# At most three loads under way on the sync queue of a one-core attention and mixing kernel

## The chip, the cores and the metric

The kernel runs on one core of a Trainium2 chip. The core has five engines that run side by side: TensorE (PE; its weight loads are listed as PEld), VectorE (DVE), ScalarE (ACT), GpSimd (POOL) and SyncE (SP). SP computes nothing; it issues transfers between the chip's memory (DRAM) and the core's own memory (SBUF). Sixteen DMA engines carry the transfers of all queues. The metric is the time of one execution in microseconds (us). Three runs before the change gave 200.77, 201.28 and 204.06 us; the median is 201.28 us.

## What is computed

There are two parts, the second fed by the first. The first is a recurrence over 768 steps for 4 batches of 8 heads with 40 channels each:

```python
for t in range(S):
    y[:, :, t] = einsum('bhd,bhde->bhe', r_t, state)
    Sa = einsum('bhde,bhe->bhd', state, a_t)
    state = state * w_t - einsum('bhd,bhe->bhde', Sa, b_t) + einsum('bhd,bhe->bhde', v_t, k_t)
```

Its output, seen as x of shape 4 x 768 x 320, goes through a mixing stage:

```python
theta = x @ w_theta
y = w_tok_r @ (x * cos(theta)) + w_tok_i @ (x * sin(theta))   # over the 768 tokens
u = x + y
out = u + maximum(u @ w_ch, 0)
```

The inputs r, k, v, w, a, b are six arrays of 4 x 8 x 768 x 40 numbers of 32 bits. They are the bulk of what is loaded.

## The kernel before, in words

**Tiles.** The 768 steps of a batch are cut into six chunks of 128 steps, so there are 24 chunks in all, each holding all eight heads. Within a chunk the recurrence is turned into matrix products; between chunks a small state is handed on. A batch's mixing stage follows when its six chunks are done, and is interleaved with the recurrence of the next batch. The products over the tokens (line 880, `chunk` in `mix_row`) are the largest group of matmuls.

**Loads.** The functions `load` and `loads` (lines 289 and 461) bring the inputs in. A chunk of one array is 160 KB. It is fetched either alone (line 464), as rows of 40 numbers, that is 160 bytes, or in pairs of chunks (line 480), as runs of 8 x 40 numbers, that is 1,280 bytes, of 320 KB. The first six chunks (`TURNED`) take k, b and a in pairs, the first eight (`RUNS`) take v in pairs, and r always comes in pairs; the rest comes in single chunks. The landing tiles are few: four for w, six for a, four for k and b together, six for v, two pairs for r. A load into a tile waits until the old contents have been read.

**Who reads the loads.** ACT takes the logarithm of w (`lw`, line 508). POOL casts k, b, a, v and r to 16 bits (line 498; the first of them on ACT, line 497), into `z`, `o`, `r` or `v`, or multiplies k, b and a by the decays (line 492, `kb` and `ah`). From there TensorE transposes them (lines 418 and 423).

**Order.** All work is recorded as operations (`plan.add`) and then issued in one long hand-kept list, `ORDER` (line 22). The list fixes the order on each engine. `HOMES` names the banks of the matmuls' memory, `PICK` the operations that take their second choice of engine, and `WARM` places small filler matmuls (line 982). The loop at line 988 goes through the list, runs each operation's function, which issues its instructions, and calls `plan.thin` (line 1000), which drops waits that another wait already covers. Each engine works through its own instructions in order and waits on semaphores for those of others.

**Queues.** SP issues 132 transfers in the list's order: 119 loads and 13 stores of the output (lines 911 and 917). Each of SP's transfers reports its landing on one of eight semaphores ("lanes"), in turn; a transfer waits until the one before it on its lane, eight transfers earlier, has landed. That is the only bound on the transfers under way that the program itself sets. POOL issues 16 loads of its own for the weights of the mixing stage (lines 926 and 934).

Of the kernel before, what the change touches and what calls it, by code (L numbers as in the profile page):

```python
# [16 lines left out]

BANKS = 8
RUNS = 8
TURNED = 6  # L20
LATE = 8
ORDER = [
# [224 lines left out]
def kernel(  # L247
# [41 lines left out]
    def load(i):  # L289
# [3 lines left out]
        def src(ap):  # L293
            return ap[bi, :, ci * C:(ci + 1) * C, :].rearrange("h t d -> t h d")
        if i < TURNED:
            return ([("raw_w", s), raw_w[s], src(w)],)
# [3 lines left out]
                [("raw_a", i % NA), raw_a[i % NA], src(a)]) + (  # L300
                () if i < RUNS else ([("raw_v", i % 6), raw_v[i % 6], src(v)],))

# [109 lines left out]
    def pair(t, g):  # L412
        return t[:, 2 * g:2 * g + 2, :].rearrange("p a b -> p (a b)")
# [14 lines left out]
    def turned(kind, kinde, i, blocks, skeys, dst, dkeys, at="tile", eng="ACT", part=64):  # L428
        p = ("ps", kind, i)
        n = len(blocks)  # L430
        whole = n <= 8
        add("PE", kind, i, lambda: turn(ps(p).bitcast(BF16), blocks), reads=skeys, writes=[p],
            at=at, new=(p, 2), alts=(("PE", lambda: turn_whole(ps(p).bitcast(BF16), blocks)),)
            if whole else (), **quad_cost(4 * n))

        def places(width, source):
            a = part * width // 64
            if len(plan.home[p]) == 2:
                return (dst_of(width).rearrange("p n (a w) -> p a n w", a=2),
                        source[:, :, 0:width * n].rearrange(  # L440
                            "p a (n w) -> p a n w", w=width)[:, :, :, 0:a])
            return (dst_of(width).rearrange("p n (a w) -> p (n a) w", a=2),
                    source[:, 0:2 * width * n].rearrange(
                        "p (n w) -> p n w", w=width)[:, :, 0:a])

        def dst_of(width):
            return dst.bitcast(FP32) if width == 32 else dst

        def words():
            to, source = places(32, ps(p))  # L450
            nc.scalar.copy(out=to, in_=source)  # L451

        def halves():
            to, source = places(64, ps(p).bitcast(BF16))
            nc.vector.tensor_copy(out=to, in_=source)
        alts = [("ACT", words), ("DVE", halves)]
        if eng == "DVE":
            alts.reverse()
        add(alts[0][0], kinde, i, alts[0][1], n * 2 * part, [p], dkeys, at=at, alts=(alts[1],))

    def loads(i):
# [7 lines left out]
        sets = [(r, raw_r[i // 2 % 2], "r")]  # L469
        if i < RUNS:  # L470
            sets.append((v, raw_o[i // 2 % 3], "o"))
        if i < TURNED:
            s = i % 4
# [16 lines left out]
    def product(kind, i, dst, in0, in1, reads, writes, fast):  # L490
        dve = ("DVE", lambda: nc.vector.tensor_tensor(out=dst, in0=in0, in1=in1, op=ALU.mult))
        pool = ("POOL", lambda: nc.gpsimd.tensor_tensor(out=dst, in0=in0, in1=in1, op=ALU.mult))  # L492
        one, two = (dve, pool) if fast else (pool, dve)
        add(one[0], kind, i, one[1], 0, reads, writes, alts=(two,))

    def cast(kind, i, dst, src, reads, writes, fast):
        act = ("ACT", lambda: nc.scalar.copy(out=dst, in_=src))
        pool = ("POOL", lambda: nc.gpsimd.tensor_copy(out=dst, in_=src))
        one, two = (act, pool) if fast else (pool, act)
        add(one[0], kind, i, one[1], 0, reads, writes, alts=(two,))  # L500

    def prep(i):
# [43 lines left out]
        fast = i < 2  # L546
        if i >= TURNED:
            product("kb", i, kb[:, :, :, 0:D], raw_kb[s4],
# [3 lines left out]
                    [("raw_a", i % NA), kwe], [("ah", i % 3)], fast)  # L552
        if i >= RUNS:
            cast("v", i, vb[:, :, 0:D], raw_v[i % 6],
# [3 lines left out]
        parts = [("f" + nm, st) for nm in "kba"]  # L558
        if i < TURNED:
            if i % 2 == 0:  # L560
# [5 lines left out]
        skeys, dkeys = [("kb", i % NKB), ("ah", i % 3)], list(parts)  # L566
        if i >= RUNS:
            blocks += [pair(vb, g) for g in range(G)]
            skeys.append(("v", i % NRV))
            dkeys.append(("vT", st))  # L570
        if i >= TURNED:
            turned("tt", "et", i, blocks, skeys, feat[:, 0:len(blocks)], dkeys)
        if i < RUNS and i % 2 == 0:
            turn_runs("o", i, o_t[i // 2 % 2], raw_o[i // 2 % 3],
# [57 lines left out]
    def turn_runs(nm, i, t, raw, dsts):  # L632
        s = i // 2 % 2
        cast(nm, i, t[:, :, :, 0:D], raw.rearrange("p c (q d) -> p q c d", q=8),
             [run_key(nm, i, 0), run_key(nm, i, 1)], [(nm, s)], i == 0)
        pr = ("ps", "t" + nm, i)
        blocks = [t[:, q].rearrange("p c d -> p (c d)") for q in range(8)]
        add("PE", "t" + nm, i, lambda: turn(ps(pr).bitcast(BF16), blocks),
            reads=[(nm, s)], writes=[pr], new=(pr, 2), **quad_cost(32))
        for x, (dst, dkey) in enumerate(dsts):  # L640
            add("ACT", "e" + nm, i + x, lambda x=x, dst=dst: nc.scalar.copy(  # L641
                out=dst.rearrange("p g (t q) -> p g t q", q=8),
                in_=ps(pr).bitcast(BF16)[:, x, 0:512].rearrange(
                    "p (q t g) -> p g t q", q=8, g=G)),
                592, [pr], [dkey])
# [328 lines left out]
    def fill(count, bank):  # L974
        f = Op()
        f.eng, f.idx, f.new = "PE", f"fill_{len(plan.known)}", None
        f.pre, f.reads, f.writes = [], (), (("ps", "fill", len(plan.known)),)
        plan.home[f.writes[0]] = (bank,)
        made = []
        nc.push_inst_callback(made.append)  # L980
        for _ in range(count):
            nc.tensor.matmul(ps(f.writes[0])[:, 0:128], lhsT=busy, rhs=busy, start=True,
                             stop=True, skip_group_check=True)
        nc.pop_inst_callback()
        plan.thin(tc, f, made)

    table = "lnexp"
    for o in plan.order():
        if o.idx in WARM:
            fill(*WARM[o.idx])  # L990
        if o.table is not None and o.table != table:
            table = o.table
            if table == "lnexp":
                nc.scalar.preload_act_table_set(LN_EXP)
        made = []
        nc.push_inst_callback(made.append)
        if o.fn is not None:
            o.fn()
        nc.pop_inst_callback()
        plan.thin(tc, o, made)  # L1000


# [28 lines left out]
```

## Time and profile before

| | |
|---|---|
| median of three runs | 201.28 us |
| profiled execution | 201.0 us |
| its span, first to last instruction | 199.3 us |
| mean granted TensorE clock | 0.987 |
| moved by DMA | 30.90 MB |
| loads of SP, 160 KB each (single chunks) | 94, of 4.4 to 4.8 us from issue to landing (medians) |
| loads of SP, 320 KB each (pairs of chunks) | 25, of 3.6 to 5.4 us (medians) |

All rows of the profile come from one execution of 201.0 us. The span is shorter by 1.7 us, because starting and ending the program lies outside it. In the lists, L464 is line 464 of the kernel; `out<-in` names the tile written and the tile read; "DMA" as the one waited for means that a transfer had not landed. In the list of waits the three numbers are the total in us, how often, and the longest. The timeline of SP gives for each transfer the time of its issue and how long the issue took; the transfer itself goes on after that. "To landing" is the time from the start of the issue to the last semaphore update. The chain of waits is followed back from the last instruction; it tells which work, end to end, set the length of the span.

### The profile page before, as it was taken

The numbers are of one execution on the slowest core, as the hardware profiler recorded it, in microseconds if no ns is written. First come the engines' busy times: TensorE is split into PE (matmuls) and PEld (weight loads), VectorE is DVE, ScalarE is ACT, GpSimd is POOL, SyncE is SP. The second block draws the span as 40 slices with busy tenths as digits, with TensorE's granted clock in tenths as the row PEclk, the third lists the DMA queues.
The fourth block names the chain that finished last, engine by engine and source line by source line (L and its number), as shares of the span: only waits on it lengthen the run. The fifth ranks groups of instructions, "written<-read, shape, count | busy, mean of one in ns | idle before, by whom it ended". The sixth has DMA issues, their size and how long they took to land.

```text
span 199.3 us, 9590 instructions
## 1 busy us (share of the span) xinstructions
PE 184.5 (93%) x4275; PEld 146.2 (73%) x4275; DVE 160.7 (81%) x265; ACT 160.7 (81%) x293; POOL 144.7 (73%) x171
## 2 busy tenths in 40 slices
PE   7879999895998898999989999999999999999992
PEld 7667787684786777777876877876877877887761
DVE  7599999994899999997988968899996647774252
ACT  3499998994999999887979898799799889894011
POOL 5347472986399999889979997764989898579100
PEclk9999999997899999999999999999999999999998
DMA  5998977999987989879988989989848301002122
GB/s 148 290 327 172 285 152 156 142 185 182 189 143 148 196 149 152 154 160 198 176 183 181 212 169 201 196 153 226 200 101 208 57 28 44 3 3 69 66 92 105
DMA packets 110312, 30.90 MB, mean 155 GB/s; under 512 B 98624, under 2 KB 110272, under 8 KB 110272
## 3 DMA queue, kind: packets, MB, share of 16 engines
q1 hardware_dynamic: 107840, 27.53, 64.7%
q0 software_dynamic: 2432, 2.77, 8.4%
q8 instruction: 33, 0.54, 1.1%
q14 instruction: 7, 0.06, 0.1%
HBM read 29.13 MB, written 3.93 MB: 166 GB/s over the span
## 4 chain that ended last, share of the span: by engine, by line
PE 70%; ACT 10%; DVE 9%; DMA 4%; issue 3%; POOL 1%; SPq 1%; POOLq 0%
PE ps L880 21%; PE ps L418 11%; PE ps L667 10%; PE ps L803 9%; PE ps L826 4%; PE ps L423 3%; DMA raw_v<-in_v_dram 2%; DVE lam L675 2%; PE ps L723 2%; DVE phi L675 2%; PE ps L744 2%; DMA raw_kb<-in_k_dram 2%; PE ps L711 2%; PE ps L706 2%; PE ps L517 2%
## 5 line engine op out<-in xcount | busy, mean ns | idle before, releaser
L880 PE MATMUL ps<-z,wtok 128*128 128x320 bf16 x288 | 48.6, 299 | 0.0
L675 DVE TENSOR_TENSOR lam<-ps,mask_p 128x1024 bf16<-128x1024 f32 x31 | 37.7, 1220 | 5.9 <-PE ps L667 5.6
L492 POOL TENSOR_TENSOR z<-cs,xp 128x640 bf16<-128x640 f32 x22 | 30.5, 1402 | 7.5 <-ACT cs L858 7.5
L880 PEld LDWEIGHTS <-wtok 128*128 128x128 bf16 x288 | 24.2, 97 | 8.7
L492 POOL TENSOR_TENSOR kb<-raw_kb,ex 128x640 bf16<-128x640 f32 x18 | 25.7, 1432 | 1.3 <-PE ps L826 0.5
L675 DVE TENSOR_TENSOR phi<-ps,mask_n 128x1024 bf16<-128x1024 f32 x19 | 23.0, 1219 | 3.2 <-PE ps L667 3.2
L675 DVE TENSOR_TENSOR psi<-ps,mask_p 128x1024 bf16<-128x1024 f32 x17 | 20.7, 1217 | 2.6 <-PE ps L667 2.6
L667 PEld LDWEIGHTS <-feat 64*128 64x128 bf16 x576 | 18.0, 95 | 6.1 <-issue 3.0
L677 ACT ACTIVATE lam<-ps 128x1024 bf16<-128x1024 f32 x17 | 17.4, 1026 | 3.6 <-PE ps L667 3.6
L679 POOL TENSOR_SCALAR_AFFINE_SELECT lam<-lam 128x1024 bf16<-128x1024 bf16 x17 | 18.6, 1095 | 0.8 <-ACT lam L677 0.7
L667 PE MATMUL ps<-feat 64*128 64x128 bf16 x384 | 17.8, 219 | 1.2 <-ACT feat L451 0.5
L826 PE MATMUL ps<-kb,lam 128*128 128x40 bf16 x384 | 15.9, 180 | 0.6 <-issue 0.5
L492 POOL TENSOR_TENSOR ah<-raw_a,ex 128x320 bf16<-128x320 f32 x18 | 14.6, 809 | 2.3 <-ACT ex L539 1.5
L826 PEld LDWEIGHTS <-lam 128*128 128x128 bf16 x384 | 13.9, 96 | 1.2 <-issue 0.6
L641 ACT COPY rT<-ps 128x512 bf16<-128x512 bf16 x24 | 13.9, 595 | 0.7 <-PE ps L418 0.7
L890 DVE TENSOR_TENSOR up<-ps,xp 128x640 bf16<-128x640 f32 x11 | 9.0, 822 | 5.3 <-PE ps L880 5.2
L451 ACT COPY feat<-ps 128x1024 f32<-128x1024 f32 (+1 forms) x13 | 12.9, 1002 | 0.5 <-PE ps L418 0.3
L451 ACT COPY uT<-ps 128x384 f32<-128x384 f32 (+1 forms) x9 | 4.0, 447 | 11.3 <-PE ps L423 7.7
L508 ACT ACTIVATE lw<-raw_w 128x320 bf16<-128x320 f32 x24 | 11.4, 479 | 1.8 <-DMA raw_w<-in_w_dram 1.8
L914 DVE SCALAR_TENSOR_TENSOR oo<-ps,up 128x640 f32<-128x640 f32 x11 | 9.0, 822 | 4.5 <-PE ps L803 4.5
L667 PE MATMUL ps<-rT,nuT 64*128 64x128 bf16 x192 | 9.7, 219 | 2.8 <-issue 2.4
L820 PE MATMUL ps<-gd,rT 128*128 128x80 bf16 x80 | 12.3, 197 | 0.0
(156 smaller groups left out, 542.9 us busy)
## 6 DMA issues: line engine op xcount, KB each, us to landing
raw_w<-in_w_dram SPq DMA_DIRECT2D x24, 160.0 KB, 4.6
raw_r<-in_r_dram SPq DMA_DIRECT2D x12, 320.0 KB, 5.0
out_dram<-oo SPq DMA_DIRECT2D x11, 320.0 KB, 3.2
raw_a<-in_a_dram SPq DMA_DIRECT2D x18, 160.0 KB, 4.8
raw_kb<-in_b_dram SPq DMA_DIRECT2D x18, 160.0 KB, 4.6
raw_kb<-in_k_dram SPq DMA_DIRECT2D x18, 160.0 KB, 4.7
raw_v<-in_v_dram SPq DMA_DIRECT2D x16, 160.0 KB, 4.4
raw_v<-in_v_dram SPq DMA_DIRECT2D x4, 320.0 KB, 5.2
```

Of the source, the lines that this page charges most:

```text
L418: nc.tensor.transpose(out=dst[:, c, n * 64:n * 64 + 64], in_=block[rows(c)], identity=ident[rows(c), rows(c)])
L451: nc.scalar.copy(out=to, in_=source)
L492: pool = ("POOL", lambda: nc.gpsimd.tensor_tensor(out=dst, in0=in0, in1=in1, op=ALU.mult))
L641: add("ACT", "e" + nm, i + x, lambda x=x, dst=dst: nc.scalar.copy(out=dst.rearrange("p g (t q) -> p g t q", q=8), in_=ps(pr).bitcast(BF16) ...
L667: nc.tensor.matmul(t[:, q, g, :], lhsT=lhs[rows(q), g, :], rhs=rhs[rows(q), g, :], start=True, stop=True)
L675: add("DVE", kindm, i, lambda: nc.vector.tensor_tensor(out=flat, in0=whole(), in1=mask.to_broadcast([128, 2 * G, 128]), op=ALU.mult), 1217 ...
L677: 1217, [p], dkeys, alts=(("ACT", lambda: nc.scalar.mul(out=flat, in_=whole(), mul=sign)),))
L679: add(None, "sel", i, None, 0, dkeys, dkeys, alts=(("POOL", lambda: nc.gpsimd.affine_select(out=flat, in_=flat, pattern=[[0, 2 * G], [1, 1 ...
L803: nc.tensor.matmul(out, lhsT=lhs[:, 3 * c + kt, :], rhs=wt[:, kt, :], start=kt == 0, stop=kt == 2)
L820: nc.tensor.matmul(t[:, g * 80:g * 80 + 80], lhsT=rT[:, g, :], rhs=gd[:, 2 * g:2 * g + 2, :], start=True, stop=False, skip_group_check=True)
L826: nc.tensor.matmul(t[:, h * D:h * D + D], lhsT=lam[:, n, p, g, :], rhs=kb[:, n, h, 0:D], start=first and n == 0, stop=n == 1, skip_group_c ...
L880: nc.tensor.matmul(to, lhsT=wtok[t % NCH][:, c, s, :], rhs=z[:, c, s], start=s == 0 and c == 0, stop=s == NT - 1 and c == 1)
```

## The change

Every load on SP, from the fourth on, gets one more dependency: on the landing of the third load ahead of it in the same queue. The list of loads is kept in `flight`. Stores on SP and the loads that POOL issues are neither counted nor held. The order of the operations, their banks and their engines stay the same.

```diff
+INFLIGHT = 3
...
+    flight = []
     for o in plan.order():
...
         if o.fn is not None:
             o.fn()
         nc.pop_inst_callback()
         plan.thin(tc, o, made)
+        if o.eng == "SP" and o.kind[0] == "l":
+            if len(flight) >= INFLIGHT:
+                tc.add_manual_dep(made[0], flight[-INFLIGHT].name, mybir.DependencyInfo(
+                    mybir.DependencyClass.Sync, mybir.DependencyReason.DATA),
+                    reason="loads in flight")
+            flight.append(made[0])
```

In the built program the lists of instructions of PE, DVE, ACT and POOL are the same as before, waits included. On SP the order is the same too. Each load waits for the lane of the third load ahead of it, and the old wait on its own lane is gone where the new one covers it, as it nearly always does. The stores lose their lane waits as well, with four exceptions near the end.

## The prediction

> **What bounds the kernel now.** I read the page first, then the chain of waits, then the list of who waited for whom, cut at 36 us, and last the issues of the sync queue (SP) one by one, because the change touches only them.
>
> ```profile
> span 199.3 us, 9590 instructions
> PE 184.5 (93%) x4275; PEld 146.2 (73%) x4275; DVE 160.7 (81%) x265; ACT 160.7 (81%) x293; POOL 144.7 (73%) x171
> q1 hardware_dynamic: 107840, 27.53, 64.7%
> PE 70%; ACT 10%; DVE 9%; DMA 4%; issue 3%; POOL 1%; SPq 1%; POOLq 0%
> ```
>
> PE carries 70% of the chain and DMA 4%, about 8 us. But q1, the queue that SP fills, uses 64.7% of the time of 16 DMA engines over the span, and the loads end well before the kernel does. So where they run, the DMA engines are nearly full. The table by stretch (length, busy time of the five engines, granted clock, DMA share, GB/s) says where:
>
> ```profile
> 8.00:24.00 16.00, 14.05 (x336) 11.16 (x335) 15.02 (x20) 15.85 (x32) 8.14 (x11) 1.00 1.02 270
> 80.00:148.00 68.00, 67.25 (x1560) 51.78 (x1552) 60.14 (x83) 58.72 (x103) 57.85 (x64) 1.00 0.94 183
> 165.00:199.00 34.00, 30.45 (x466) 22.91 (x466) 18.46 (x25) 16.90 (x32) 15.83 (x15) 0.98 0.15 50
> ```
>
> DMA share is 1.02 at the start and 0.94 in the middle, while PE is busy 67.25 of 68.00 us there. In the last 34 us hardly a load is left (0.15), so the change can't act there. Who waits for loads, up to 36 us and then after it:
>
> ```profile
> POOL o L498 <- DMA raw_v<-in_v_dram: 6.3, 2, 5.2
> POOL z L498 <- DMA raw_kb<-in_k_dram: 3.7, 2, 1.9
> POOL z L498 <- DMA raw_kb<-in_b_dram: 3.2, 2, 3.0
> POOL z L498 <- DMA raw_a<-in_a_dram: 2.5, 2, 1.7
> ACT z L497 <- DMA raw_kb<-in_b_dram: 2.2, 1, 2.2
> ```
>
> ```profile
> POOL r L498 <- DMA raw_r<-in_r_dram: 1.1, 1, 1.1
> POOL kb L492 <- DMA raw_kb<-in_b_dram: 0.4, 1, 0.4
> POOL v L498 <- DMA raw_v<-in_v_dram: 0.3, 1, 0.3
> ```
>
> Up to 36 us these five sum to 17.9 us; from there to 160 us all DMA waits sum to 1.8 us. Loads therefore set the pace at the start, and arrive just early enough later.
>
> **The change, part by part.** It adds no instruction of work and moves none: each load's own issue waits until the third load ahead of it has landed. Stores are not counted and get no such wait. Behind a waiting load stand all later loads and stores, since SP issues in order; every consumer on ACT and POOL waits for them. The old waits on a reused completion lane, eight transfers back, fall away, and they cost nothing, being long over.
>
> How many loads are under way now follows from these rows of SP's timeline (start, duration of the issue) and of the list of issues in windows holding one load each (last number: us from issue to landing):
>
> ```profile
> 0.80 0.72 SPq L480 DMA_DIRECT2D raw_kb<-in_b_dram  x1
> 1.58 0.61 SPq L480 DMA_DIRECT2D raw_kb<-in_k_dram  x1
> 2.24 0.60 SPq L464 DMA_DIRECT2D raw_w<-in_w_dram  x1
> 2.88 0.60 SPq L480 DMA_DIRECT2D raw_a<-in_a_dram  x1
> ...
> 18.81 0.61 SPq L480 DMA_DIRECT2D raw_a<-in_a_dram  x1
> ```
>
> ```profile
> raw_kb<-in_b_dram SPq DMA_DIRECT2D x1, 320.0 KB, 3.5
> raw_kb<-in_k_dram SPq DMA_DIRECT2D x1, 320.0 KB, 3.7
> raw_a<-in_a_dram SPq DMA_DIRECT2D x1, 320.0 KB, 4.8
> raw_w<-in_w_dram SPq DMA_DIRECT2D x1, 160.0 KB, 4.5
> ```
>
> ```profile
> raw_a<-in_a_dram SPq DMA_DIRECT2D x1, 320.0 KB, 4.6
> ```
>
> Call the loads 0, 1, 2, ... The first lands at 0.80 + 3.5 = 4.3, the next at 5.3, load 2 at 6.7, and load 3, issued at 2.88, at 7.7. With the change load 3 is issued at 4.3, 1.4 us later. Whether it also lands later depends on how long a load takes when little is ahead of it. Two rows, from windows with one transfer each, bound that: a 160 KB load issued near 25 us, after SP had waited for a buffer, and a store near 163 us that had the DMA engines to itself:
>
> ```profile
> raw_w<-in_w_dram SPq DMA_DIRECT2D x1, 160.0 KB, 2.6
> ```
>
> ```profile
> out_dram<-oo SPq DMA_DIRECT2D x1, 320.0 KB, 2.3
> ```
>
> So of the 4.5 to 5 us that a load now takes, about 2 are time in the queue, and that part can be given up for nothing. Three under way at C us each land one every C/3.
>
> *First stretch, to 24 us.* From load 3 (7.7) to load 19 (18.81 + 4.6 = 23.4) there are 16 loads in 15.7 us: 0.98 each, 2.94 per three. With C = 2.6 the wait is hidden (0.87 each). With C = 3.5, load 0's own time and its size, each takes 1.17 and load 19 lands 3.0 later. These loads are mostly of 320 KB; between 2.6 and 3.5 I take the middle, 3.05: 1.02 each, +0.6 at load 19. To this I add 0.2, because a semaphore is complete only when the slowest of 16 engines is, and the quicker ones then run dry sooner. Not all reaches the chain: in 8:24 ACT is busy 15.85 of 16.00 us, and it covers part of the delay as long as the chain runs through it. Taken: **+0.5**; ends 0 and +2.5.
>
> *The raw_v load at 28.80.* It stands in the chain by itself:
>
> ```profile
> 28.39 0.37 SPq L464
> ...
> 28.80 4.90 DMA raw_v<-in_v_dram
> ...
> 33.76 1.39 POOL o L498 x2
> ```
>
> ```profile
> 25.40 0.74 SPq L480 DMA_DIRECT2D raw_r<-in_r_dram  x1
> ...
> 28.80 1.86 SPq L480 DMA_DIRECT2D raw_v<-in_v_dram  x1
> ```
>
> ```profile
> raw_r<-in_r_dram SPq DMA_DIRECT2D x1, 320.0 KB, 5.4
> ```
>
> The third load ahead of it is raw_r, landing at 25.40 + 5.4 = 30.8. Now the issue runs from 28.80 to 30.66, for 1.86 us where a free one after a wait takes 0.37: the hardware itself holds SP until the queue has room. With the change it runs from 30.8 to 31.2, so it ends 0.5 later, not 2. If raw_r lands later too, up to 1 more. POOL has nothing else to do (it waited 5.2), so all of it goes to the chain: **+0.8**, ends 0 and +1.6.
>
> *From 36 us on.* Long issues show that the hardware does already most of what the change asks for:
>
> ```profile
> 52.67 0.58 SPq L464 DMA_DIRECT2D raw_w<-in_w_dram  x1
> 53.29 3.00 SPq L464 DMA_DIRECT2D raw_v<-in_v_dram  x1
> 56.38 0.66 SPq L464 DMA_DIRECT2D raw_kb<-in_k_dram  x1
> ```
>
> The issue at 53.29 hung for 3.00 us. What the loads need here, from the queue's row for 100:148:
>
> ```profile
> q1 hardware_dynamic: 39903, 8.85, 91.2%
> ```
>
> 8.85 MB are as much as 54 transfers of 160 KB in 48 us: one every 0.89 us, three every 2.67. A load with little ahead takes 2.6, plus 0.05 for SP to wake (my estimate, from raw_v: it landed at 28.80 + 4.90 = 33.70, and POOL began at 33.76): 2.65. That is as tight as it can be without loss. About every second load would be issued later than now by up to 0.7, and three consumers had no slack at all, as the waits of 1.1, 0.4 and 0.3 show. Taken: **+1.0** for those and for the slip behind them; ends 0 and +6 (second rival).
>
> The profiled execution took 201.0 us, 1.7 around its span; the median of the three runs is 201.28, so the sum holds for both. 201.0 + 0.5 + 0.8 + 1.0 = **203.3 us**.
>
> A rule speaks against these additions. The Trainium skill ("DMA: Bandwidth & Descriptors", section "Anatomy of one DMA — SWDGE (gpsimd) path") gives a transfer a fixed part of about 2.0 us plus bytes at 436 GB/s; that is given for another kind of queue, and an estimate from it is 2.4 us for 160 KB and 2.8 for 320 KB. The trace's 2.6 and 2.3 lie near it. By it three loads land every 2.4 to 2.8 us, less than 2.94 at the start, and the sum would be about +0.5, the first rival below.
>
> **The rivals.** *It costs nothing.* For it: the long issues (1.86, 3.00), which mean that a fourth load is only half in the queue anyway, and C = 2.6. Against it: the first rows, in which load 3's issue at 2.88 isn't held at all, and raw_v's 0.5. Time: 201.0 + 0.5 = 201.5. That the wait isn't there at all would give the same time; but in the built program each load from the fourth on names the lane of the third ahead of it, and the lists of the other engines are as before.
>
> *The queue runs dry.* Place: 80 to 148 us, DMA share 0.94, so 4 us in 68 are free to make up for gaps. It decides from C over 2.67: at 3.05, my value for the start, three loads take 0.38 longer, and the 54 transfers of 100:148 slip by 18 x 0.38 = 6.8 us. With a little from 80:100 and from the start, and about 2 us of slack ahead of most consumers taken off, +7: 208. For it: no spare share, PE in a fixed order, and 16 DMA engines that don't finish together. Against it: a wait that replaces a hung issue (3.00) adds only the difference.
>
> *Faster.* Instruction loads and POOL's weight loads share the DMA engines, and a shorter SP queue could let them by. A wait of PE, and q8, the queue of the instruction loads, over the span and then in 165:199:
>
> ```profile
> PE ps L667 <- issue: 2.4, 1, 2.4
> ```
>
> ```profile
> q8 instruction: 33, 0.54, 1.1%
> ```
>
> ```profile
> q8 instruction: 4, 0.07, 0.9%
> ```
>
> PE once sat 2.4 us with nothing to wait for but its own issue; the chain has 3% of "issue", 6 us. Halved, that gives 198. Against it: an instruction packet takes 0.011 x 16 x 199.3 / 33 = 1.06 us over the span and 0.009 x 16 x 34 / 4 = 1.2 in 165:199, where SP's queue is nearly empty, so the queue doesn't slow the packet itself. The Trainium skill ("DMA: Bandwidth & Descriptors", section "Queues, rings and completion order") says that a DMA engine takes turns between queues packet by packet, so a deep SP queue would hold another queue up by one packet only; by this rule nothing is gained.
>
> **How the numbers follow.** The forecast, +1 to +6 around 203.3, gets 0.45; 2% of the median is 4.0 us, about what a measurement of this kernel can tell from no change, so some 0.13 of it lies over 205.3. No cost: 0.18. The queue runs dry, 204.5 to 213: 0.30, all but a sliver slower. Faster: 0.07, of which 0.05 is under 197.3. That gives slower 0.43, same 0.52, faster 0.05. The range leaves out the faster case and the top third of the dry queue: 200.0 to 209.0.
>
> **What would show it.** Right: median time to landing of the 160 KB loads falls to 3 to 3.5; hung issues vanish and SP's own waits name raw loads; POOL's waits for loads up to 36 us grow from 15.7 by 1 to 2; raw_v lands near 34.5; DMA share in 80:148 stays over 0.9. Wrong: if DMA share there falls to 0.85 and POOL or ACT wait for loads for several us after 36, the queue runs dry; if time to landing falls and no wait grows, it costs nothing; if "issue" shrinks in the chain, the third rival has it.

## The result and the profile after

The changed kernel takes **215.15 us** (median of six runs, 213.82 to 216.54) against 201.03 us for the kernel before in the same call (200.04 to 204.06): ratio **1.071, interval 1.065 to 1.077**. That is slower by 14 us, and over the upper end of the predicted range. The profiled execution took 215.14 us. Here and below, ratios count undisturbed executions only, medians count all of them.

The page of the changed kernel (line numbers of the loads and their readers are now one higher):

```profile
span 213.4 us, 9586 instructions
PE 188.7 (88%) x4275; PEld 148.3 (69%) x4275; DVE 160.8 (75%) x265; ACT 160.9 (75%) x293; POOL 144.8 (68%) x171
q1 hardware_dynamic: 107840, 27.53, 61.9%
DMA 45%; PE 44%; ACT 5%; POOL 2%; issue 1%; SPq 1%; DVE 0%; POOLq 0%
```

DVE, ACT and POOL did the same work in the same busy time. DMA went from 4% of the chain of waits to 45%. The table by stretch, with the same columns as in the prediction:

```profile
8.00:24.00 16.00, 12.79 (x276) 9.73 (x276) 12.58 (x18) 13.46 (x28) 7.09 (x9) 0.89 0.86 201
80.00:148.00 68.00, 61.34 (x1435) 47.01 (x1428) 51.64 (x72) 51.70 (x94) 53.94 (x60) 0.95 0.86 159
179.00:213.00 34.00, 30.56 (x473) 22.90 (x466) 18.52 (x26) 17.01 (x32) 15.95 (x15) 0.98 0.15 51
```

DMA share fell from 1.02 to 0.86 at the start and from 0.94 to 0.86 in 80:148, and in 80:148 PE is busy 61.34 of 68.00 us where it was 67.25. The last 34 us, with hardly a load in them, look as before: what was lost came earlier and was carried to the end.

Where it was lost shows when the start of the n-th matmul is compared in the two traces (same instructions in the same order, so each difference is a lag; worked out from the instruction records):

| time in the trace before, us | 15 | 23 | 31 | 39 | 55 | 72 | 88 | 105 | 113 | 122 | 131 and later |
|---|---|---|---|---|---|---|---|---|---|---|---|
| lag of PE after the change, us | 1.9 | 2.8 | 5.3 | 6.6 | 5.8 | 6.1 | 5.8 | 7.5 | 8.0 | 14.1 | 14.1 |

There are two stretches: +6.6 by 39 us, and +8.3 between 88 and 122. Between them the lag stands still. In a second trace of the same kernel (the run beside the fillers, below) the first is 7.2, and the second is spread out: 5.7 at 88 us, 6.5 at 113, 8.7 at 122, 12.4 at 140, 12.6 at 165. So where in the late stretch the loss is taken differs from one execution to the next.

SP's timeline at the start and at raw_v:

```profile
2.25 0.60 SPq L465 DMA_DIRECT2D raw_w<-in_w_dram  x1
4.39 0.60 SPq L481 DMA_DIRECT2D raw_a<-in_a_dram  x1
5.31 0.39 SPq L465 DMA_DIRECT2D raw_w<-in_w_dram  x1
...
35.80 0.61 SPq L481 DMA_DIRECT2D raw_v<-in_v_dram  x1
```

Load 3 goes out at 4.39, when load 0 has landed, and no longer at 2.88. The raw_v load that went out at 28.80 goes out at 35.80; it lands at 40.26 (33.71 before). Its issue no longer hangs: 0.61 us, where it was 1.86. Over all of SP's transfers, issues of more than 1.5 us went from 23 to 4. The page's list of issues (count, size, median us to landing):

```profile
raw_w<-in_w_dram SPq DMA_DIRECT2D x24, 160.0 KB, 3.6
...
raw_a<-in_a_dram SPq DMA_DIRECT2D x18, 160.0 KB, 4.1
```

A 160 KB load with two ahead of it takes **3.6 to 4.1 us**, where the forecast took 3.05 for the first stretch and 2.65 from 36 us on. Who waited for loads, up to 42 us and after that (the largest rows of such waits):

```profile
POOL o L499 <- DMA raw_v<-in_v_dram: 6.3, 2, 5.3
POOL z L499 <- DMA raw_kb<-in_k_dram: 4.8, 2, 3.0
POOL z L499 <- DMA raw_a<-in_a_dram: 4.6, 3, 2.2
ACT lw L509 <- DMA raw_w<-in_w_dram: 3.0, 3, 1.4
ACT z L498 <- DMA raw_kb<-in_b_dram: 2.3, 1, 2.3
POOL r L499 <- DMA raw_r<-in_r_dram: 1.4, 1, 1.4
```

```profile
ACT lw L509 <- DMA raw_w<-in_w_dram: 5.1, 2, 4.5
POOL z L493 <- DMA raw_w<-in_w_dram: 4.6, 1, 4.6
POOL ah L493 <- DMA raw_a<-in_a_dram: 3.2, 2, 2.2
POOL kb L493 <- DMA raw_kb<-in_b_dram: 1.7, 1, 1.7
PE ps L804 <- DMA wch<-in_moe_w_ch_dram: 1.7, 1, 1.7
```

Early on these waits grew by only a few us, though everything is 6.6 us late by then: a lag of PE that goes round through ACT, DVE and POOL shows as their waiting for PE (15.3 us up to 42 us, where it was 2.5 up to 36), not for loads. Later, where before there were 1.8 us of waits for loads, there are single ones of 4.5 and 4.6. And PE itself once waits 1.7 us for `wch`, one of POOL's weight loads; the larger load of `wch` took 8.7 us to land, 6.5 before.

The chain of waits of the changed kernel, by start and duration:

```profile
88.38 3.98 DMA raw_kb<-in_b_dram
92.36 0.02 issue
92.37 3.69 DMA raw_r<-in_r_dram
...
96.13 10.44 DMA raw_kb<-in_k_dram
106.57 0.02 issue
106.59 4.25 DMA raw_a<-in_a_dram
...
122.94 4.36 DMA raw_w<-in_w_dram
127.30 0.02 issue
127.33 0.47 ACT lw L509
```

From 78 to 127 us the chain holds nothing but load after load, each issued as the third ahead of it lands. No engine works in it: the round trip of a load sets the pace. The 10.44 us lie where POOL issues six weight loads of its own.

### The profile page after: what moved, and what is told of

Read it like the earlier page. It is cut to its first block, busy times and chain, and to the rows that moved or that the text cites. A ratio compares the mean times of both kernels' runs of the same rounds, so it can differ in the third digit from the quotient of the medians.

```text
span 213.4 us, 9586 instructions
## 1 busy us (share of the span) xinstructions
PE 188.7 (88%) x4275; PEld 148.3 (69%) x4275; DVE 160.8 (75%) x265; ACT 160.9 (75%) x293; POOL 144.8 (68%) x171
## 4 chain that ended last, share of the span: by engine, by line
DMA 45%; PE 44%; ACT 5%; POOL 2%; issue 1%; SPq 1%; DVE 0%; POOLq 0%
PE ps L881 14%; DMA raw_w<-in_w_dram 12%; DMA raw_a<-in_a_dram 9%; DMA raw_kb<-in_k_dram 8%; PE ps L804 6%; PE ps L419 6%; DMA raw_r<-in_r_dram 6%; PE ps L668 6%; DMA raw_kb<-in_b_dram 6%; DMA raw_v<-in_v_dram 4%; PE ps L827 2%; PE ps L424 2%; PE ps L724 1%; PE ps L745 1%; PE ps L712 1%
## 5 line engine op out<-in xcount | busy, mean ns | idle before, releaser
L881 PE MATMUL ps<-z,wtok 128*128 128x320 bf16 x288 | 50.2, 305 | 1.4 <-POOL z L493 1.1
L881 PEld LDWEIGHTS <-wtok 128*128 128x128 bf16 x288 | 24.8, 99 | 10.7 <-issue 1.6
L668 PEld LDWEIGHTS <-feat 64*128 64x128 bf16 x576 | 18.6, 97 | 6.5 <-issue 3.7
L668 PE MATMUL ps<-feat 64*128 64x128 bf16 x384 | 18.5, 224 | 1.1 <-ACT feat L452 0.5
L452 ACT COPY uT<-ps 128x384 f32<-128x384 f32 (+1 forms) x9 | 4.0, 447 | 12.4 <-PE ps L424 8.8
L804 PE MATMUL ps<-wch,uT 128*128 128x320 bf16 x72 | 11.7, 299 | 1.7 <-DMA wch<-in_moe_w_ch_dram 1.7
L718 ACT CAST nx<-ps 128x320 bf16<-128x320 f32 x24 | 10.2, 426 | 3.8 <-PE ps L712 3.7
```

What stands on the lines that cost most here:

```text
L668: nc.tensor.matmul(t[:, q, g, :], lhsT=lhs[rows(q), g, :], rhs=rhs[rows(q), g, :], start=True, stop=True)
L804: nc.tensor.matmul(out, lhsT=lhs[:, 3 * c + kt, :], rhs=wt[:, kt, :], start=kt == 0, stop=kt == 2)
L881: nc.tensor.matmul(to, lhsT=wtok[t % NCH][:, c, s, :], rhs=z[:, c, s], start=s == 0 and c == 0, stop=s == NT - 1 and c == 1)
```

## The experiments

**How many may be under way.** Three runs change only the limit, a fourth lets one load at a time go, in the first stretch alone, to measure a lone load.

```diff
-INFLIGHT = 3
+INFLIGHT = 2
```

> The limit is two loads instead of three. Theory (a load's round trip, from the issue to the landing that releases the next issue, is some 3.7 us with two loads ahead of it, so that the number under way divided by the round trip sets the pace): with one load ahead the round trip falls only to about 3.0, the pace is 1.5 us per load, 119 loads end near 185 us and 42 us of work follow: 225 to 240 us. Rival (each added wait costs a fixed price, of SP waking and of the wait itself, whatever the distance): as many waits as with three, so 215 us, within 3.

Measured: 251.68 us (245.41 to 252.14; before 199.97), more than the theory's 225 to 240; its pace of 1.5 us per load was 1.79 at the start.

```diff
-INFLIGHT = 3
+INFLIGHT = 4
```

> The limit is four. Theory: four under way in 3.9 to 4.6 us are one per 0.98 to 1.15, about what the kernel before does by itself (0.98 at the start): 201 to 205 us, so most of the 14 us is gone. Rival (a fixed price for each wait): 215 us, within 3, as with three.

Measured: 200.49 us, ratio 1.003 (0.999 to 1.007).

```diff
-INFLIGHT = 3
+INFLIGHT = 6
```

> The limit is six, which the kernel before reaches only in its first 20 us. Theory: no difference from the kernel before, 200.5 to 202 us. Rival (a fixed price for each wait): 210 us or more. Third reading (a little less crowding helps the other queues): under 200 us here or with four.

Measured: 200.55 us, ratio 1.002 (0.996 to 1.007).

```diff
-INFLIGHT = 3
+INFLIGHT = 1
...
-            if len(flight) >= INFLIGHT:
+            if INFLIGHT <= len(flight) < 28:
```

> Each of the first 28 loads waits for the one just ahead, so that it travels alone; the rest is free. It measures the round trip with nothing ahead. Forecast's value: 2.6 us for 160 KB and up to 3.5 for 320 KB, so 28 loads take some 85 us. If a load alone takes as long as the 3.6 to 4.1 that it takes in the changed kernel, the time is in the way and not in the queue: 105 us. The kernel as a whole: about 250 to 275 us.

Measured: 254.53 us (one run). The lone loads, from SP's timeline (start and duration of the issue; each starts as the one before it has landed) and from the list of issues up to 88 us:

```profile
4.19 0.61 SPq L481 DMA_DIRECT2D raw_kb<-in_k_dram  x1
7.42 0.41 SPq L465 DMA_DIRECT2D raw_w<-in_w_dram  x1
9.93 0.60 SPq L481 DMA_DIRECT2D raw_a<-in_a_dram  x1
13.13 0.39 SPq L465 DMA_DIRECT2D raw_w<-in_w_dram  x1
```

```profile
raw_w<-in_w_dram SPq DMA_DIRECT2D x10, 160.0 KB, 2.5
raw_v<-in_v_dram SPq DMA_DIRECT2D x4, 320.0 KB, 3.3
```

A lone 160 KB load takes 2.5 us (7.42 to 9.93; two of the twelve took 3.6 and 4.2), a lone 320 KB load 3.1 to 3.7, mostly 3.3. So the forecast's 2.6 and 3.5 were right for a load that is alone. They were not the time of a load with two others under way. The five limits side by side (pace: landing of load 19 less that of load 3, by 16; share: DMA share in 8:24; medians to landing of raw_w over the whole kernel, of the first ten for one; hung issues: SP's issues of more than 1.5 us, counted in the traces):

| loads under way | one | two | three | four | six | before |
|---|---|---|---|---|---|---|
| raw_w, us to landing | 2.5 | 3.0 | 3.6 | 4.4 | 4.9 | 4.6 |
| pace at the start, us per load | 3.22 | 1.79 | 1.34 | 1.13 | 1.00 | 0.98 |
| DMA share in 8:24 | 0.38 | 0.62 | 0.86 | 0.92 | 0.98 | 1.02 |
| hung issues | (first stretch only) | 2 | 4 | 22 | 28 | 23 |
| kernel, us | (first stretch only) | 251.68 | 215.15 | 200.49 | 200.55 | 201.03 |

Up to four, each further load under way adds 0.5 to 0.8 us to the round trip and still speeds up the pace. With three the engines stand still for a part of each round trip, and yet each load queues behind two others: both at once. With four the pace is some 15% slower than the free one and the time is as before, so the kernel's edge lies between three and four. With three SP's issues hardly ever hang; with four they hang about as often as without a limit. A fixed price per added wait is ruled out: four and six add nearly as many waits as three and cost nothing.

**Which stretch pays.** Seven runs hold only some of the loads, the condition being the only edit; the diff shows the first, the others put the range named in place of it.

```diff
-            if len(flight) >= INFLIGHT:
+            if INFLIGHT <= len(flight) < 28:
```

*First stretch, loads 3 to 27.*

> The limit of three holds for the first 28 loads alone, which fill the time up to 34 us in the kernel before; later loads are free. Theory: load 19 lands 6 us later as with the whole change, raw_v on the chain likewise, and nothing makes up for it later, since PE is busy 67 of 68 us in the middle: 206 to 208 us. Rival (the loss is made in the long middle, as the forecast's second rival had it, and the start is absorbed by slack): 201 to 203 us.

Measured: 204.96 us (before 199.97), ratio 1.022 (1.014 to 1.029).

*Everything from load 28 on* (`len(flight) >= 28`).

> The limit of three holds from load 28 on alone; the first 28 loads are free. With the limit on the first 28 alone the kernel took 5.0 us more, with the whole change 14.1. If the stages add up (each load stream late by its own stage, and nothing downstream takes it back): 209 to 210 us. If the late start is what makes the later loads collide (a shifted order against POOL's weight loads), the rest by itself costs little: 201 to 204 us.

Measured: 204.99 us (before 201.11), ratio 1.020 (1.010 to 1.030).

*Loads 28 to 67* (`28 <= len(flight) < 68`).

> The limit of three holds for loads 28 to 67 alone, some 35 to 90 us in the kernel before. By the landings of the changed kernel, the lag behind the kernel before grows there from 6.5 to some 7 to 8 us only, since for long stretches POOL's weight loads fill the DMA engines. Round-trip theory: 201 to 203 us. If every wait costs alike (40 of the 91 waits behind load 28, which cost some 9 us together): 205 us.

Measured: 201.19 us (before 201.11), ratio 1.005 (0.999 to 1.011).

*Loads from 68 on* (`len(flight) >= 68`).

> The limit of three holds from load 68 on alone, from some 87 us in the kernel before. There the lag grows from some 7 to 16 us by the landings, with PE busy nearly all the time and the loads at one per 0.89 us. Round-trip theory: 206 to 209 us, most of what the limit costs behind the start. If the waits cost alike: 205 us; if these consumers have enough slack: 201 to 203 us.

Measured: 203.38 us (before 201.11), ratio 1.012 (1.003 to 1.021).

Of these four forecasts only the one for loads 28 to 67 came in; the first stretch cost 1 us less than its theory said, the late one 2.6 less, and everything from load 28 on lay between theory and rival. So each stretch alone costs 0 to 5 us, and the parts sum to 7 to 9, not 14. I had two explanations: the burst of POOL's weight loads in the middle of the late stretch, and a reserve that all stretches share. The next four runs were on one chip (before: 199.90).

*All held but loads 70 to 75*, those that are issued during the burst.

```diff
-            if len(flight) >= INFLIGHT:
+            if len(flight) >= INFLIGHT and not 70 <= len(flight) < 76:
```

> Held as in the changed kernel, except loads 70 to 75, those that are issued while POOL's six weight loads of 88 to 92 us are in the DMA engines; they go out as early as before. Theory (the burst): a limit of three costs most where three loads stand behind POOL's burst and nothing more may be queued; with the six exempt the jump of PE's lag from 8 to 14 us shrinks to 2 or less, and the time is 207 to 210 us. Rival (steady pace): the loads are late by 7 to 8 us from the first stretch on and three per 3.6 to 4.8 us are too slow anyway; the jump comes as before, 213 to 216.

Measured: 215.38 us, ratio 1.076 (1.067 to 1.086). **The burst theory falls:** with the six free the time is the same. PE's lag climbs (7.5 at 113 us, 9.8 at 122, 11.4 at 140, 12.4 at 165) instead of jumping at one place, but so it does in the second trace of the changed kernel, with nothing freed; the climb can't be put down to the six loads.

*First stretch and late stretch* (`INFLIGHT <= len(flight) < 28 or len(flight) >= 68`).

> Held: loads 3 to 27 and those from 68 on; loads 28 to 67 as before the change. Alone the two stretches cost about 4 and 2.3 us. Theory (shared slack): a late first stretch uses up the few us by which later loads come early, so the sum is more than its parts: 211 to 215. Rival (they add up): 206.5 to 208.5. If it stays under 206, the slack is regained between 36 and 80 us.

Measured: 212.72 us, ratio 1.066 (1.055 to 1.077).

*First stretch and loads 68 to 77* (`INFLIGHT <= len(flight) < 28 or 68 <= len(flight) < 78`).

> Held: loads 3 to 27 and 68 to 77, which are issued from POOL's third burst to the next ten loads. Theory (the burst): nearly as slow as the run with all loads from 68 on held, within 1.5 us of it. Rival (steady pace): ten loads can't do it; as the first stretch alone, 204.5 to 206.

Measured: 208.25 us (206.31 to 212.59), 4.5 less than the run before it and between the two forecasts. The ten loads at the burst make at most a part of the late loss: in the trace PE's lag grows by 1.3 us behind 88 us, where it grows by 5.0 in the run before.

*First stretch and loads from 78 on* (`INFLIGHT <= len(flight) < 28 or len(flight) >= 78`).

> Held: loads 3 to 27 and those from 78 on, after POOL's third burst has landed. Theory (the burst): as the first stretch alone, 204.5 to 206.5. Rival (steady pace): the loads fall behind at 1.2 to 1.4 us each against 0.9 needed, so 208 to 214.

Measured: 211.87 us, ratio 1.057 (1.045 to 1.068). By these medians the steady pace, after the burst has landed, makes most of it; the trace, of the quickest of four executions, shows only 2.2 us of it.

**Is the clock a cause?** After stalls the profile shows TensorE at half clock. The table by stretch of the kernel before (length, busy time of five engines, clock, DMA share, GB/s), and then of the changed one:

```profile
46.00:48.00 2.00, 0.23 (x6) 0.23 (x7) 0.09 (x1) 0.00 (x0) 0.88 (x2) 0.88 1.09 199
48.00:51.00 3.00, 3.00 (x78) 2.51 (x75) 1.75 (x2) 2.41 (x4) 1.72 (x2) 0.51 0.73 125
```

```profile
52.00:54.00 2.00, 0.20 (x8) 0.20 (x9) 0.64 (x1) 0.17 (x1) 1.33 (x1) 1.00 1.18 226
54.00:58.00 4.00, 4.00 (x116) 3.54 (x110) 2.84 (x3) 3.39 (x6) 1.81 (x2) 0.57 0.84 145
...
124.00:126.00 2.00, 0.41 (x16) 0.38 (x17) 0.95 (x1) 0.00 (x0) 2.00 (x3) 1.00 1.15 179
...
128.00:134.00 6.00, 4.88 (x78) 3.27 (x80) 1.70 (x2) 3.90 (x7) 4.29 (x5) 0.58 0.95 193
```

PE stands nearly still for 2 us, and is then granted half clock for 3.4 us, once for 6.8 (the traces' clock records). The changed kernel has more such places, and PE's busy time is 4.2 us longer (188.7 against 184.5). The next run fills the waits with small matmuls whose results nobody uses.

```diff
 WARM = {
...
-    592: (1, 3)}
+    592: (1, 3), 33: (12, 6), 210: (24, 0), 221: (16, 0), 302: (24, 6), 905: (16, 0), 1082: (20, 4)}
```

> The changed kernel, with 112 more small filler matmuls that compute nothing which is used (WARM at operations 33, 210, 221, 302, 905 and 1082), put where its trace shows TensorE waiting 1.3 to 2.5 us; each is about 0.06 us at full clock, so they run inside the waits. Theory (the clock is a cause): after each such wait the trace shows 4 to 7 us at half clock; with the waits filled the clock stays at 1.00 there, and of the 14 us, 3 to 5 go: 210 to 212.5. Rival (the clock is only a companion, since PE has to wait for the next load anyhow): the granted clock rises, the time stays within 1.5 us of the changed kernel's. Second rival: the fillers cost their own time, up to 4 us slower.

Measured: 215.32 us (before 201.56), ratio 1.069 (1.060 to 1.077). Beside it on the same chip the changed kernel as it is:

> The changed kernel as it is, as the measure for the run with fillers beside it on the same chip: 213 to 216, ratio 1.065 to 1.077.

Measured: 214.94 us, ratio 1.069 (1.060 to 1.079). The table by stretch of the run with fillers:

```profile
52.00:54.00 2.00, 2.00 (x56) 1.85 (x50) 0.96 (x1) 0.67 (x3) 1.60 (x3) 1.00 0.82 176
54.00:58.00 4.00, 3.59 (x126) 2.80 (x122) 3.24 (x3) 3.73 (x7) 1.73 (x2) 1.00 0.92 154
...
128.00:134.00 6.00, 6.00 (x149) 4.46 (x146) 5.15 (x6) 4.79 (x10) 3.72 (x5) 1.00 0.81 168
```

The clock is back at 1.00 in these places (two spells of half clock remain in this trace, at 11.7 and 42.4 us). Span times (1 - mean clock), the us that the throttle took, went from 7.7 to 2.8 on the mean of four executions each. The time did not follow: 215.32 (214.04 to 216.55) against 214.94 (213.66 to 216.36). **The gain of 3 to 5 us did not come.** As I read it, PE waits for the next load anyhow, and at half clock it waits less. A gain of some 2 us isn't excluded: the executions spread by that much, and in this trace 24 of the fillers stand in the chain of waits themselves, with 1.45 us. The Trainium skill ("TensorE: Matmul & The Clock Gate", section "Terms") puts the penalty of the gate at the throttled time times the share of pulses withheld. Read as time of the kernel, these 4.9 us would have come back; the two medians don't show it.

The same idea in the kernel before, at its one such place:

```diff
 WARM = {
...
-    592: (1, 3)}
+    592: (1, 3), 302: (24, 6)}
```

> The kernel before, with 24 fillers ahead of operation 302 only, where its own trace shows TensorE busy 0.23 of 2.00 us and then 3 us at a granted clock of 0.51. Theory (the clock is a cause): 1 to 1.5 us faster, ratio 0.992 to 0.996. Rival (companion): same, 0.997 to 1.003; the fillers cost, 1.003 to 1.007.

Measured: 201.84 us, ratio 1.002 (0.998 to 1.006). This one says nothing on the clock: its table by stretch shows the stall and the half clock as they were,

```profile
46.00:48.00 2.00, 0.20 (x3) 0.20 (x3) 0.34 (x1) 0.00 (x0) 1.12 (x2) 0.89 1.17 214
48.00:51.00 3.00, 3.00 (x37) 2.61 (x35) 0.00 (x0) 0.33 (x1) 0.64 (x1) 0.50 0.75 135
```

because the fillers did not run inside it: in the trace four start by 45.6 us and the other twenty from 47.8 to 49.8, and their median duration is 0.314 us, that of half clock, where it is 0.219 in the run with 112 fillers.

**Do the stretches add up?** First and late stretch had cost 5.0 and 2.3 us alone, in two calls, and 12.8 together in a third. So all three once more on one chip (before: 199.66).

> Held: loads 3 to 27 only, side by side with the next two kernels on one chip. If the stretches interact (shared slack), as measured alone before: 204 to 206, ratio 1.015 to 1.028. If the earlier figure was a low draw: 206 to 208, ratio 1.03 to 1.04.

> Held: loads from 68 on only. If the stretches interact: 202.5 to 204.5, ratio 1.008 to 1.018. If the earlier figure was a low draw: 205 to 207, ratio 1.025 to 1.035.

> Held: both stretches, loads 28 to 67 free. If they interact: 211 to 215, at least 3 us more than the sum of the two runs beside it. If they only add up: the sum of the two within 2 us.

Measured: first stretch 206.88 us (+7.2; ratio 1.028, 1.022 to 1.035), late stretch 203.95 (+4.3; 199.75 to 207.71), both 209.32 (+9.7; 205.08 to 212.80). By the medians the sum of the two is 11.5, and both together cost 9.7: **side by side these two stretches only add up.** Executions of one kernel spread by 4 to 8 us here, and the first series lay on different chips; whether its 12.8 came from that, no run shows. For the late stretch the ratio (1.004, 0.998 to 1.011) rests on 3 of 12 executions, so I read its price as 0 to 4 us.

What is left for loads 28 to 67, which cost nothing alone, is 14.1 less 9.7 to 12.8, so 1.3 to 4.4 us. The traces show a way for it. For each load I took the time from its landing to its first reader; the median over loads 68 to 79 is the reserve with which the late stretch begins. The second row is how much further PE falls behind the trace before in the late stretch, worked out as in the table of lags; each figure is one execution:

| held | nothing | first | late | first and late | middle | all from load 28 on | all but the burst | all (two traces) |
|---|---|---|---|---|---|---|---|---|
| reserve of loads 68 to 79, us | 5.3 | 5.6, 7.4 | 4.4, 5.4 | 4.2, 4.9 | 2.5 | 3.6 | 2.6 | 1.3, 2.2 |
| growth of PE's lag from 88 to 165 us | | 0.2, 0.0 | 6.0, 4.8 | 3.9, 5.0 | 1.6 | 4.6 | 7.2 | 8.3, 6.9 |

Wherever the middle is held the reserve is down to 1.3 to 3.6. My reading was that a late stretch that falls back then hands nearly all of it to PE, and that the middle alone has free loads behind it that make up for it. That this reserve is the cause is only argued: no run moved it by itself, and the run with everything from load 28 on held doesn't bear it out, since PE falls back there by 4.6 us, no more than with the late stretch alone. It falls back by about 7 to 8 only where all three stretches are held. Why it takes all three stays open.

## Why the prediction was wrong

- **What bounds the kernel** was read rightly: full DMA engines where the loads run, loads just early enough, nothing to lose in the last 34 us.
- **"So of the 4.5 to 5 us that a load now takes, about 2 are time in the queue, and that part can be given up for nothing."** This step failed. The ends were right (2.6 and 3.5; lone loads measured 2.5 and 3.1 to 3.7), but they belong to a load that is alone. "Three under way at C us each" needs C with two others ahead, and that is 3.6 to 4.1, over my upper end of 3.5, where the sum had 3.05 and 2.65. Of the 2 us, only about 1 went.
- **First stretch, +0.5 (ends 0 and +2.5).** Load 19 landed at 29.75 instead of 23.38, 6.4 later, and PE was 6.6 late at 39 us. By the forecast's own formula C = 3.9 (the mean of loads 3 to 19 in the trace after) gives 1.30 per load; measured were 1.34. So the formula held and C was mis-sized. No run separates the 0.2 that I added for the slowest of 16 engines.
- **The raw_v load, +0.8.** Its landing moved by 6.6, as much as the loads ahead of it (6.9 at load 22): it added nothing of its own. That a wait in place of a hung issue costs only the difference was right here.
- **From 36 us on, +1.0 (ends 0 and +6).** Measured +7.5 (lag 6.6 to 14.1), in the second trace +5.4. "Long issues show that the hardware does already most of what the change asks for" was wrong by one load: the limit that changes nothing is four, and three is under it. In the trace before, the 21 hung issues behind 28 us start with three or four earlier transfers of SP still under way and end with two or three left; counting them would have shown it.
- **"One every 0.89 us, three every 2.67"** was wrong too, the other way. It counts bytes, and the limit counts loads. In the rows for 100:148 five of the loads are pairs, which count double there, and four transfers are stores, which nothing holds:

```profile
raw_r<-in_r_dram SPq DMA_DIRECT2D x5, 320.0 KB, 4.3
...
out_dram<-oo SPq DMA_DIRECT2D x4, 320.0 KB, 3.8
```

SP issues 40 loads there in 48 us: one every 1.2 us, three every 3.6. By that the 2.65 and even the 3.05 of the forecast would have cost nothing, two under way at 3.0 are too slow, three at 3.6 to 4.1 lie at the edge or over it, and four at 4.4 (1.1 each) are quick enough, as the limits showed.

- **The rival "the queue runs dry"** named the right place and the right mechanism. That its price (+7) fits that stretch is in part luck, since its C of 3.05 and its threshold of 2.67 were both too low. With C = 3.9 its formula would give 18 x (3.9 - 2.67) = 22 us; with 40 loads and a need of 3.6 it gives 13 x 0.3 = 4 (my estimate), against 5.4 to 7.5 measured. It took the first stretch at almost nothing, hence 208 and not 215.
- **"It costs nothing"** is out. **"Faster"** too: "issue" shrank from 3% to 1% of the chain, but because loads took its place. POOL's weight loads landed no sooner: 6.2 and 5.7 us on the median for the two groups of 192 KB, 5.7 and 5.8 before.
- **The rule of the Trainium skill** with a fixed part and a rate ("DMA: Bandwidth & Descriptors", section "Anatomy of one DMA — SWDGE (gpsimd) path") came near the lone loads (2.4 and 2.8 estimated, 2.5 and 3.3 measured). It has no term for other loads under way, so it couldn't carry the sum.
- **The signs.** Hung issues went, as said. Time to landing fell only to 3.6 to 4.1, not to 3 to 3.5, and raw_v landed at 40.26, not near 34.5. POOL's waits for loads went from 16.0 (15.7 without one of 0.3 for raw_r) up to 36 us to 17.4 up to 42, the growth of 1 to 2 that I gave as a sign of being right, though the lag was 6.6: that sign was a bad one. The two signs for "wrong", DMA share near 0.85 in 80:148 and single waits of several us after 36, both showed.

## What to carry to other kernels

The time of a transfer that is alone is not its time with two others under way: what a limit of n costs follows from the round trip at n, and it holds n back as soon as that round trip divided by n is longer than the time that the consumers leave per transfer. That need is counted in the unit of the limit, here loads and not bytes. A hung issue shows that the hardware has a limit, not which; before setting one, count how many transfers are really under way when an issue hangs, and stay at or above that. A stretch that loses nothing by itself may still have spent some of the reserve of the next one; in this kernel that it did is seen, and what it cost is not.

## What the runs showed of the hardware

- One load at a time, of 160 or 320 KB, keeps the sixteen DMA engines busy for 0.38 of the time (8 to 24 us); with at most two, three, four and six under way it is 0.62, 0.86, 0.92 and 0.98.
- In this kernel the queue holds SP's issues by itself from about the fourth transfer on: 4 issues of more than 1.5 us with at most three loads under way, 22 with four, 28 with six, 23 without a limit. In the first 16 us of the kernel before, where most loads are pairs, the two such issues had five and six transfers ahead of them; behind 28 us three or four. A single load makes 1,024 packets of 160 bytes in the traces and a pair 256 of 1,280; whether the bound goes by loads or by packets no run separates.
- After waits of 0.8 to 2.5 us PE was granted half clock for 3.4 us, once for 6.8; in the 3.4 us ahead of each such spell it had been busy for 1.1 to 2.2 us (the traces of the kernel before, of the changed one twice and of it with fillers, their ends left out). I had not looked at the clock for the forecast; filling such waits raised the mean clock and left the time where it was, within some 2 us.
